# First forward block of a convolution kernel: zeros multiplied while x loads, casts on two engines, two products taken directly in quarters

## The chip, the cores and the metric

The kernel runs on one core of a Trainium2 chip. A core has a matrix engine (TensorE, PE in the profile; its weight loads are PEld), a vector engine (VectorE, DVE), a scalar engine (ScalarE, ACT), a general engine (GpSimd, POOL) and a queue engine that issues DMAs (SyncE, SP). Each works its own list of instructions in order and waits on semaphores for the others. The metric is the device time of one execution in microseconds (us), as the median of the runs.

## The reference

A stride-2 convolution over time, a normalisation over time and a GELU, and the gradients of all of it:

```python
L = (T - K) // 2 + 1                      # x is [2, 16000, 256], w is [31, 256, 256], bf16
h = sum(x[:, i:i + 2 * L:2, :] @ w[i] for i in range(K))
h = (h - mean_over_time(h)) / sqrt(var_over_time(h) + 1e-5)
out = gelu(h * gn_gamma + gn_beta)        # and the gradients of x, w, gamma, beta for grad_out
```

The outputs are `out`, the gradient of x, the gradient of w, and those of gamma and beta. The change touches only the first piece of the forward convolution.

## The kernel before

**The whole.** The program has three parts: the forward convolution (stages F0 to F7: 2 batches, 4 chunks each), the element-wise work and the input gradient (G0 to G7), and the weight gradient (W0 to W8). Each convolution is done with fewer products than its definition has: sums and differences of shifted inputs are multiplied by differences of weights, and the results are added up. A chunk has three branches, called `B_`, `A` and `C_` and worked in this order (`ORDER`); each branch has three products ("leaves") of the same names. A branch's operands are sums of rows of x that DVE makes (`f_sums`, line 468), and its weights are differences of the taps in `w` that DVE makes too (`w_sub`, line 460).

**Two forms of a product.** The direct form is `f_leaf` (line 512): 64 matmuls of 256 columns for a whole leaf (two rows of the output, two halves of the channels, four taps, two parities and two halves of the input channels), and its operand is the sum as it is. The other form has three parts: `f_three_b` (line 524), 16 matmuls with a difference of weights `WD`, after which ACT copies that result negated into the other half of the PSUM tile; and `f_three_ac` (line 540), 32 matmuls onto both halves with one more sum, `third`, as operand. It takes 48 matmuls, one more DVE sum, one more DVE difference of weights, and the ACT copy between its parts.

**The first block** (`f_first`, line 705) is branch `B_` of the first chunk. Nothing is in SBUF when it starts. `x_load` (line 390) loads the odd columns of 272 rows of x as plain rows in three pieces (128, 128 and 16 rows; `rows`), has the 31 taps of `w` loaded by 16 loads (`load_w`, line 439; leaf A's in `load_w(A)`, leaf C's in `load_w(C_)`, each for one half of the input channels, one parity and one of two tap groups), transposes the x rows on PE against an identity matrix (`x_first`, line 412), and loads the even columns with four DMA transposes (`turn`, line 304). In `x_first` PE transposes both pieces of 128 rows into four PSUM tiles, ACT casts each tile to bf16 in one piece of 1024 elements (`put`, line 419), and the 16 rows follow. Then `f_first` makes the weights of branch `B_` (the subtractions `w_sub` in quarters or halves), the sums `la` and `lc` (`second`, line 495), and computes leaf A directly (64 matmuls, in three pieces: a quarter, a quarter and a half) and leaves C and B in the other form (48 each). Three ACT passes (`keep`) and a DVE sum end it. The next branch (`split`, line 653) starts with a sum over all columns of x, the even ones included, and an `f_three_b`.

**What sets the order.** Every operation is recorded in a plan by `add` (line 170): engine, cost, what it reads and writes, and a function that emits it. The plan is emitted in the order of the list `STEPS` (line 39), which holds the differences of successive operation numbers; `order` (line 199) adds them up, and `emit` (line 208) pins the program to that order. So each engine's instructions stand in the order of the list, over the whole program. The planner that wrote the list is not part of the kernel; the costs and slacks handed to `add` are not used at run time. Where several operations are recorded by one helper, the profile shows the helper's line: L509 is every forward matmul, L462 every `w_sub`, L477 every sum in `f_sums`, L422 the casts in `x_first`, L538 the copy in `f_three_b`, L562 the `keep` passes.

Of the kernel before, what the change touches and what calls it, by code (L numbers as in the profile page):

```python
# [13 lines left out]
ALU = mybir.AluOpType  # L14
# [20 lines left out]
def mmt(n):  # L35
    return n / 2400.0 + 0.0025
# [1587 lines left out]
```

## Time and profile before

| | us |
|---|---|
| median of 3 runs | 1102.59 (1102.41 to 1102.68) |
| the profiled execution, its own time | 1101.5 |
| its span from the first instruction to the last | 1099.5 |
| PE busy | 1078.2 (98%) |
| DVE busy | 995.2 (91%) |
| ACT busy | 610.5 (56%) |
| POOL busy | 10.3 (1%) |
| mean granted TensorE clock | 0.999 |

The span is 2.0 us shorter than that execution's time: what lies around the program. In the rows that follow, a timeline row gives the start, the length, the engine, the line, the operation with its tiles and shapes, and how often it stands there in a row; the bracket gives the idle time of the engine before it and what ended it. A row of waits gives the total, the number of times, and the longest. A row of groups gives the count, the busy time, the mean of one in nanoseconds, and the idle time before them. The tile `arena` is all of the kernel's large SBUF storage, and `ps` are the four PSUM tiles (`ring`).

### The profile page before, as it was taken

How to read it: one execution, taken by the hardware profiler on the slowest of the kernel's cores; microseconds unless marked ns; L12 is line 12 of the kernel's file. 1: busy time of each engine (PE TensorE's matmuls, PEld its weight loads, DVE VectorE, ACT ScalarE, POOL GpSimd, SP SyncE). 2: the span in 40 equal slices, each digit the busy share in tenths (PEclk: the TensorE clock that was granted, in tenths of full speed). 3: DMA queues.
4: the chain of work that ended last, by engine and by line, in shares of the span. 5: the costliest groups of instructions: out<-in, count | busy, mean ns of one | idle time of the engine just before them, and what ended most of it. 6: DMA issues, size and time to landing. Idle time of an engine off the chain costs nothing. (4 is left out here: it accounts for less than half of the span.)

```text
span 1099.5 us, 19714 instructions
## 1 busy us (share of the span) xinstructions
PE 1078.2 (98%) x8132; PEld 794.9 (72%) x8132; DVE 995.2 (91%) x1026; ACT 610.5 (56%) x854; POOL 10.3 (1%) x27
## 2 busy tenths in 40 slices
PE   5999999999999999999999999999999999998998
PEld 4888899988888994444444444444478888887887
DVE  5987787899989997999999998989699999999995
ACT  2335444678887649798866676676643323331332
POOL 0000000000001000000000000000000000000000
PEclk9999999999999999999999999999999999999999
DMA  9499989796969698988595999989898565796674
GB/s 233 70 206 271 254 254 259 211 203 164 256 150 195 180 320 284 267 230 280 162 286 165 313 308 345 264 255 314 271 332 208 185 221 168 255 356 224 224 235 135
DMA packets 346892, 261.46 MB, mean 238 GB/s; under 512 B 187702, under 2 KB 315572, under 8 KB 340916
## 3 DMA queue, kind: packets, MB, share of 16 engines
q1 hardware_dynamic: 346612, 260.22, 83.6%
q8 instruction: 63, 1.03, 0.4%
q14 instruction: 25, 0.20, 0.1%
q0 software_dynamic: 192, 0.00, 0.0%
HBM read 120.00 MB, written 94.86 MB: 195 GB/s over the span
## 5 line engine op out<-in xcount | busy, mean ns | idle before, releaser
L509 PE MATMUL ps<-arena 128*128 128x256 bf16 (+3 forms) x3668 | 394.9, 271 | 13.7 <-DVE arena L462 7.1
L1057 PE MATMUL ps<-arena 128*128 128x512 bf16 (+1 forms) x1872 | 400.0, 376 | 0.6 <-ACT ps L1084 0.3
L509 PEld LDWEIGHTS <-arena 128*128 128x128 bf16 x3668 | 358.2, 98 | 50.2 <-DVE arena L462 7.9
L1057 PEld LDWEIGHTS <-arena 128*128 128x128 bf16 x1872 | 183.3, 98 | 216.9 <-issue 1.5
L562 ACT ACTIVATE arena<-ps 128x1024 bf16<-128x1024 f32 x189 | 191.2, 1022 | 243.9 <-PE ps L1348 125.3
L1348 PE MATMUL ps<-arena 128*128 128x256 bf16 x2592 | 283.5, 273 | 2.9 <-DVE arena L1301 2.1
L1348 PEld LDWEIGHTS <-arena 128*128 128x128 bf16 x2592 | 253.4, 98 | 33.1 <-DVE arena L1301 2.5
L477 DVE TENSOR_TENSOR arena<-arena 128x2064 bf16<-128x2064 bf16 (+8 forms) x132 | 164.1, 1266 | 22.2 <-PE ps L509 19.6
L1301 DVE TENSOR_TENSOR arena<-arena 128x4096 bf16<-128x4096 bf16 (+2 forms) x50 | 107.1, 2165 | 0.1
L861 DVE TENSOR_TENSOR arena<-arena 128x2048 bf16<-128x2048 bf16 (+1 forms) x80 | 95.4, 1194 | 4.9 <-ACT arena L853 2.4
L1084 ACT ACTIVATE ps<-ps 128x512 f32<-128x512 f32 x108 | 63.0, 584 | 45.3 <-PE ps L1057 45.0
L1020 DVE TENSOR_TENSOR arena<-arena 128x1032 bf16<-128x1032 bf16 (+7 forms) x111 | 85.0, 795 | 0.5 <-PE ps L1057 0.2
L1099 DVE TENSOR_TENSOR arena<-arena 128x1024 bf16<-128x1024 bf16 (+1 forms) x70 | 63.3, 913 | 16.7 <-ACT arena L562 16.5
L849 ACT ACTIVATE arena<-arena,stats 128x1024 bf16<-128x1024 bf16 (+1 forms) x64 | 74.6, 1208 | 2.5 <-DVE stats L795 2.5
L1311 DVE TENSOR_TENSOR arena<-arena 128x4096 bf16<-128x4096 bf16 x32 | 72.5, 2283 | 1.3 <-PE ps L1348 1.2
L1243 DVE TENSOR_TENSOR arena<-arena 128x1536 bf16<-128x1536 bf16 (+3 forms) x56 | 62.0, 1122 | 7.0 <-DMA arena<-dnd 4.8
L1420 ACT COPY ps<-ps 128x512 f32<-128x512 f32 x54 | 30.5, 570 | 62.4 <-PE ps L1348 62.4
L1407 DVE TENSOR_TENSOR arena<-arena 128x2048 bf16<-128x2048 bf16 x54 | 63.7, 1216 | 0.0
L462 DVE TENSOR_TENSOR arena<-arena 128x2048 bf16<-128x2048 bf16 (+1 forms) x45 | 51.0, 1147 | 13.4 <-DMA arena<-in_w_dram 10.8
L538 ACT ACTIVATE ps<-ps 128x512 f32<-128x512 f32 x59 | 34.3, 582 | 49.7 <-PE ps L509 49.6
L584 ACT ACTIVATE arena<-ps 128x512 bf16<-128x512 f32 (+1 forms) x64 | 36.9, 582 | 38.7 <-PE ps L509 38.6
L1354 DVE TENSOR_TENSOR arena<-arena 128x1024 bf16<-128x1024 bf16 x75 | 49.0, 682 | 8.7 <-ACT arena L562 8.5
(68 smaller groups left out, 462.3 us busy)
## 6 DMA issues: line engine op xcount, KB each, us to landing
arena<-in_x_dram SPq DMA_DIRECT2D x28, 1024.0 KB, 8.4
arena<-d2d SPq DMA_DIRECT2D x16, 1216.0 KB, 8.6
out_dram<-arena SPq DMA_DIRECT2D x35, 512.0 KB, 4.9
d2d<-arena SPq DMA_DIRECT2D x30, 384.0 KB, 7.7
arena<-dnd SPq DMA_DIRECT2D x10, 960.0 KB, 7.2
arena<-vl SPq DMA_DIRECT2D x9, 1024.0 KB, 9.7
arena<-in_x_dram SPq DMA_DIRECT2D x32, 256.0 KB, 4.1
hd<-arena SPq DMA_DIRECT2D x8, 1024.0 KB, 5.5
```

Of the source, the lines that this page charges most:

```text
L477: lambda: nc.vector.tensor_tensor(out=o, in0=a, in1=b, op=ALU.add))
L509: yield nc.tensor.matmul(ps[:, dh, cs], lhsT=wt, rhs=mv, start=s0, stop=False, skip_group_check=True)
L562: lambda: nc.scalar.activation(out=out, in_=ps, func=ACT.Copy, scale=scale))
L849: lambda o=o, func=func, i=h[:, dh], sc=sc, bi=bi: SC.activation(out=o, in_=i, func=func, bias=bi, scale=sc))
L861: add("DVE", dve(8 * wd), [o], [a, b_], lambda: V.tensor_tensor(out=o, in0=a, in1=b_, op=op))
L1020: lambda: nc.vector.tensor_tensor(out=o, in0=a, in1=b, op=ALU.add))
L1057: yield nc.tensor.matmul(ps[:, e, 0:wide], lhsT=lt, rhs=mv, start=s0, stop=False, skip_group_check=True)
L1099: add("DVE", dve(o.free_size(), rate), [o], [a, b], lambda: nc.vector.tensor_tensor(out=o, in0=a, in1=b, op=op))
L1301: add("DVE", dve(o.free_size()), outs, ins, lambda: nc.vector.tensor_tensor(out=o, in0=a, in1=b, op=op), kind=kind + " weight_grad")
L1311: add("DVE", dve(4096), [o], [a, b], lambda: nc.vector.tensor_tensor(out=o, in0=a, in1=b, op=ALU.add))
L1348: yield nc.tensor.matmul(ps[:, s, c0:c1], lhsT=lt, rhs=mv, start=s0, stop=False, skip_group_check=True)
L1407: add("DVE", dve(2048), [d4], [d], lambda: nc.vector.tensor_tensor(out=d4, in0=fan(d[:, o0:o0 + 3 * s + 1:s, :], 1, (o1 - o0) * D), in1=fa ...
```

## The change

In the start-up and in `f_first`:

- The tile of zeros `zt2` is set by DVE as the first operation, no longer by POOL. A new helper `idle` multiplies zeros by zeros: eight matmuls of 512 columns at the start of PE's list, before x is there, and six of 512 columns behind the last transposition of x. Their results are not used.
- The casts of the transposed x go in eight pieces of 512 elements, four behind each piece of 128 rows; of each four, three are on ACT and the last on DVE.
- Leaf C is now computed directly as leaf A is (64 matmuls in place of 48, with no `third` and no `WD` for it at this place), and both leaves go in four quarters, one for each half of the input channels and each parity. The subtraction that a quarter needs is a step of its own. The sums `la`, `lc` and the `third` of leaf B are made in two halves each.
- Leaf B keeps the other form.
- `STEPS` is a new list for the whole program (3178 operations, 3164 before). In it x is loaded first, then the weights of leaf A in the pairs that one subtraction needs, then those of leaf C in the same way; the first steps of PE after leaf C are leaf B's `f_three_b`, its `f_three_ac`, and the next branch's `f_three_b` and `f_three_ac`, with no other PE step between.

```diff
+    add("DVE", 0.3, [zt2[:]], [], lambda: nc.vector.memset(zt2[:], 0.0))
     add("DVE", 0.1, [eps_t[:]], [], lambda: nc.vector.memset(eps_t[:], EPS))
...
-    add("POOL", 0.4, [zt2[:]], [], lambda: nc.gpsimd.memset(zt2[:], 0.0))
...
+        def idle(ps, n, cols, fresh, slow):
+            jobs = [(k,) for k in range(n)]
+
+            def go():
+                for _ in jobs:
+                    yield nc.tensor.matmul(ps[:, 0:cols], lhsT=zt2[:, 0:P], rhs=zt2[:, 0:cols], start=fresh, stop=False, skip_group_check=True)
+            return add("PE", n * mmt(cols) * slow, [ps[:, 0:cols]], [zt2[:, 0:cols]], go)
...
         slots = (2, 3, 0, 1)
+        idle(ring[1][:, 1], 8, 512, True, 2.0)
         for g in range(2):
             for j in range(4):
                 for dh in range(2):
-                    pe_turn(ring[slots[j]], dh, [(256 * (r % 2) + P * g, g, P, j, r) for r in (2 * dh, 2 * dh + 1)], g == 0)
-        for j in range(4):
-            ps = ring[slots[j]]
-            k = 4 * (2 * j + 1)
-            put("ACT", flat[:, k:k + 4, 0:256], ps[:].rearrange("p a (r f) -> p (a r) f", r=2))
+                    pe_turn(ring[slots[j]], dh, [(256 * (r % 2) + P * g, g, P, j, r) for r in (2 * dh, 2 * dh + 1)], g == 0, 2.0 - g)
+            for j in range(4):
+                k = 4 * (2 * j + 1)
+                put("DVE" if j == 3 else "ACT", flat[:, k:k + 4, P * g:P * g + P],
+                    ring[slots[j]][:].rearrange("p a (r f) -> p (a r) f", r=2)[:, :, P * g:P * g + P])
         ps = ring[2]
-        pe_turn(ps, 0, [(16 * (4 * j + r), 2, 16, j, r) for j in range(4) for r in range(4)])
+        last = pe_turn(ps, 0, [(16 * (4 * j + r), 2, 16, j, r) for j in range(4) for r in range(4)])
...
+        plan.ops[idle(ring[3][:, 1], 6, 512, True, 1.0)]["preds"].add(last)
...
     def f_first(xt):
-        for sl in (A, C_):
+        ops, third, second = f_sums(xt, 0, 0, B_, 0)
+        for lf in (A, C_):
             for ch in range(2):
-                for v in ([slice(None)] if ch or sl == C_ else [0, 1]):
-                    w_sub(*(W[br][:, sl, ch, :, v] for br in (B_, C_, A)))
-        ops, third, second = f_sums(xt, 0, 0, B_, 0)
-        second(A)
-        second(C_)
+                for par in range(2):
+                    w_sub(*(W[br][:, lf, ch, :, par] for br in (B_, C_, A)))
+            second(lf)
...
-        third(C_, U[2])
-        third(B_, U[1])
         pa, pc, pb = ring[0], ring[1], ring[3]
-        f_leaf(pa, B_, A, ops[A], 0, HM, HM, True, (0,), (0,), 2.0)
-        f_leaf(pa, B_, A, ops[A], 0, HM, HM, False, (0,), (1,))
-        f_leaf(pa, B_, A, ops[A], 0, HM, HM, False, (1,))
-        for ps, lf, u in ((pc, C_, U[2]), (pb, B_, U[1])):
-            f_three_b(ps, B_, lf, ops[lf], 0, HM)
-            f_three_ac(ps, B_, lf, u, 0, HM, HM)
+        for ps, lf in ((pa, A), (pc, C_)):
+            for ch in range(2):
+                for par in range(2):
+                    f_leaf(ps, B_, lf, ops[lf], 0, HM, HM, ch + par == 0, (ch,), (par,))
+        f_three_b(pb, B_, B_, ops[B_], 0, HM)
+        f_three_ac(pb, B_, B_, U[1], 0, HM, HM)
```

The `third(B_, U[1])` now stands behind the differences of branch `B_`. The helper in `f_sums` makes its sums in two halves where the new flag `halves` is set (the first block alone).

More of the change, by code (lines that the diff above doesn't have):

```diff
@@ L412, in x_first, with pe_turn @@
     def x_first(flat, rows):
-        def pe_turn(ps, dh, parts, fresh=True):
+        def pe_turn(ps, dh, parts, fresh=True, slow=1.0):
             jobs = [(dh, slice(c0, c0 + nm), rows[g][0:nm, j, r * P:(r + 1) * P], ident[0:nm, 0:nm], fresh and i == 0)
                     for i, (c0, g, nm, j, r) in enumerate(parts)]
-            f_mm(ps, jobs, [ps[:, dh]], [ident, *(rows[g] for g in sorted({p[1] for p in parts}))], 2.0)
+            return f_mm(ps, jobs, [ps[:, dh]], [ident, *(rows[g] for g in sorted({p[1] for p in parts}))], slow)
+        def idle(ps, n, cols, fresh, slow):
[4 more added lines that the diff above has]
+            return add("PE", n * mmt(cols) * slow, [ps[:, 0:cols]], [zt2[:, 0:cols]], go)
         def put(eng, o, i):
@@ L468, in f_sums @@
     def f_sums(xt, b, c, br, li):
+        halves = (b, c, br) == (0, 0, B_)
         def tt(n, o, a, b, x=0):
@@ L475, in tt @@
                 b = cross(b, 1)
-            add("DVE", dve(o.free_size()), [o], [a, b],
-                lambda: nc.vector.tensor_tensor(out=o, in0=a, in1=b, op=ALU.add))
+            for e in range(2) if halves else (slice(None),):
+                e = slice(e, e + 1) if halves else e
+                p, q, r = o[:, e], a[:, e], b[:, e]
+                add("DVE", dve(p.free_size()), [p], [q, r],
+                    lambda p=p, q=q, r=r: nc.vector.tensor_tensor(out=p, in0=q, in1=r, op=ALU.add))
         if br == B_:
@@ L495, in second @@
         def second(lf):
-            if lf == A and (b, c, br) == (0, 0, B_):
-                for e in range(2):
-                    tt(260, *(v[:, e:e + 1] for v in (la, E0, E1)))
-            elif lf == A:
+            if lf == A:
                 tt(260, la, E0, E1)
@@ L509, in go @@
                 yield nc.tensor.matmul(ps[:, dh, cs], lhsT=wt, rhs=mv, start=s0, stop=False, skip_group_check=True)
-        add("PE", sum(mmt(j[1].stop - j[1].start) for j in jobs) * slow, outs, ins, go)
+        return add("PE", sum(mmt(j[1].stop - j[1].start) for j in jobs) * slow, outs, ins, go)
     def f_leaf(ps, br, lf, op, co, we, wo, fresh, chs=(0, 1), pars=(0, 1), slow=1.0):
@@ L717, in f_first @@
             w_sub(WD[br, B_], v[:, :, 1:4:2], v[:, :, 0:4:2])
+            if br == B_:
+                third(B_, U[1])
         for br in (A, C_, B_):
```

151 rows, old and new, of the table STEPS are left out of this document.

## The prediction

> **What bounds the kernel now.** I read the page's head first, then who waited for whom on PE, then PE's instructions in order of time, then busy time by stretch.
>
> ```profile
> span 1099.5 us, 19714 instructions
> PE 1078.2 (98%) x8132; PEld 794.9 (72%) x8132; DVE 995.2 (91%) x1026; ACT 610.5 (56%) x854; POOL 10.3 (1%) x27
> ```
> ```profile
> PE ps L509 <- DVE arena L462: 7.1, 3, 5.2
> PE ps L509 <- DMA arena<-in_x_dram: 6.3, 2, 4.5
> PE ps L1348 <- DVE arena L1301: 2.1, 1, 2.1
> PE ps L1348 <- DVE arena L1407: 0.8, 1, 0.8
> PE ps L509 <- DVE arena L477: 0.3, 1, 0.3
> PE ps L1057 <- ACT ps L1084: 0.3, 1, 0.3
> PE ps L1057 <- ACT arena L562: 0.3, 1, 0.3
> ```
> ```profile
> 4.53 1.25 PE L509 MATMUL ps<-arena 128*128 128x128 bf16 x10 [4.53 <-DMA arena<-in_x_dram]
> 7.57 3.05 PE L509 MATMUL ps<-arena 128*128 128x128 bf16 x38 [1.79 <-DMA arena<-in_x_dram]
> 15.86 3.60 PE L509 MATMUL ps<-arena 128*128 128x256 bf16 x16 [5.24 <-DVE arena L462]
> 19.82 1.93 PE L509 MATMUL ps<-arena 128*128 128x256 bf16 x16 [0.36 <-DVE arena L462]
> 23.22 56.96 PE L509 MATMUL ps<-arena 128*128 128x256 bf16 x518 [1.48 <-DVE arena L462]
> ```
> ```profile
> 23.22:60.00 36.78, 36.78 (x336) 32.73 (x337) 36.78 (x34) 10.71 (x19) 0.00 (x0) 1.00 0.58 99
> 930.00:1001.00 71.00, 68.14 (x623) 60.47 (x621) 70.90 (x53) 21.09 (x26) 0.00 (x0) 1.00 0.84 289
> ```
>
> PE is busy for 1078.2 of 1099.5 us. Of its 21.3 idle, 4.53 + 1.79 + 5.24 + 0.36 + 1.48 = 13.4 lie before 23.22. After that 2.1 + 0.8 + 3 x 0.3 = 3.8 are waits, and the rest is the end. So from 23.22 on the time is a count of matmuls, and the question is how far PE has come when it first runs without a break. A matmul of 256 columns then takes 56.96/518 = 0.110. The stretch from 23.22 to 60 (its columns are length, then PE, PEld, DVE, ACT, POOL busy) shows DVE just as full: it can become the next bound.
>
> **The mark.** Before, the first block has 64 + 48 + 48 = 160 products, and 32 of them (two groups of 16) are behind PE at 23.22. The other 128 cost 128 x 0.110 = 14.1: PE has worked them off at 37.3 (a few of the next branch run between them, which moves no sum).
>
> **When the first weight pair is there.**
>
> ```profile
> 11.56 1.23 DVE L462 TENSOR_TENSOR arena<-arena 128x2048 bf16<-128x2048 bf16 x1 [9.97 <-DMA arena<-in_w_dram]
> 12.70 1.30 DVE L477 TENSOR_TENSOR arena<-arena 128x1040 bf16<-128x1040 bf16 x2
> 16.67 10.02 DVE L462 TENSOR_TENSOR arena<-arena 128x2048 bf16<-128x2048 bf16 x9 [0.87 <-DMA arena<-in_w_dram]
> ```
> ```profile
> arena<-in_w_dram SPq DMA_DIRECT2D x14, 256.0 KB, 5.6
> arena<-in_x_dram SPq DMA_DIRECT2D x2, 512.0 KB
> arena<-in_w_dram SPq DMA_DIRECT2D x2, 192.0 KB, 5.3
> arena<-in_x_dram SPq DMA_DIRECT2D x1, 64.0 KB, 6.5
> arena<-in_x_dram SPq DMA_TRANSPOSE x4, 4.2
> ```
>
> In the old list the DVE step at 11.56 waits for x (1088 KB) and four weight loads (960 KB), 2048 KB; the one at 16.67 for ten weight loads, 3520 KB. That is 1472 KB in 5.11, 288 KB per us. The new list loads x, then the weights in the pairs that one subtraction needs, leaf A first. The first pair is complete at 1600 KB: 11.56 - 448/288 = 10.0. The last is complete at 5056 KB: 16.67 + 1536/288 = 22.0; the pairs between come every 1.8 (the last half of them a little faster).
>
> **The start of the products.** Leaf A's first quarter needs its subtraction (1024 elements) and both halves of the sum `la`.
>
> ```profile
> L462 DVE TENSOR_TENSOR arena<-arena 128x1024 bf16<-128x1024 bf16 x2 | 1.4, 688 | 0.0
> L477 DVE TENSOR_TENSOR arena<-arena 128x1040 bf16<-128x1040 bf16 x2 | 1.3, 694 | 0.0
> L1099 DVE TENSOR_TENSOR arena<-ps,arena 128x1024 bf16<-128x1024 f32 x24 | 29.2, 1215 | 0.8 <-ACT arena L849 0.6 <-PE ps L1057 0.2
> ```
> ```profile
> 8.21 4.04 ACT L422 CAST arena<-ps 128x1024 bf16<-128x1024 f32 x5 [6.19 <-PE ps L509]
> 28.78 0.58 ACT L538 ACTIVATE ps<-ps 128x512 f32<-128x512 f32 x1 [0.82 <-PE ps L509]
> ```
>
> Two short DVE steps take 1.30 one after the other, 0.61 from start to start: 10.0 + 0.61 + 0.69 + 0.61 = 11.9, and with the handover PE starts at 12.0 instead of 15.86. The casts lie under this: x's second half is in at 7.57, three ACT casts of 512 elements at 0.58 end by about 9.7, the small one by 10.1, against a need at 10.6. The fourth cast, on DVE, no row shows. Half of the 1.215 of a 1024-element step that reads PSUM is 0.61, an ACT cast 0.58, the whole 1.22; I take 0.68. DVE idles there until 10.0, so it costs nothing below 1.3.
>
> **The clock.** The 16 matmuls at 15.86 took 3.60, the next 16 took 1.93: PE comes slow out of a pause of 5.24 and stays fast over pauses of 0.36 and 1.48. This excess of 1.67 goes if the zeros keep PE running. Eight of 512 columns at the slow pace (3.60/16 per 256) last 3.6, from about 1.1 to 4.7, when x lands anyway (4.53); six at the fast pace last 1.3, behind the transposes, to about 10.5. The pause left before 12.0 is 1.5, like the one of 1.48. On the path the first eight cost at most 0.2, ahead of a wait for x of 1.79, so nothing; the last six wait for the remaining transposes and for one cast, and queued behind them on PE is leaf A's first quarter, which is not ready before 12.0. [...]
>
> **The sum.** The block now has 64 + 64 + 48 = 176 products, 19.4 at 0.110: 12.0 + 19.4 = 31.4. The order list adds two stalls. In the old list the second product's `f_three_b` stands between the first's and its `f_three_ac`, and covers the ACT copy that `f_three_ac` needs. Now one product of this form is left, and nothing on PE stands between; nor does it for the next branch's first product, which the old list covers with leftovers. Each stall is the copy of 0.58 and the handovers. From below 0.6, from above 0.9; I take 0.85, since a matmul's own length exceeds its pace by 0.16.
>
> ```profile
> L509 PE MATMUL ps<-arena 128*128 128x256 bf16 (+3 forms) x3668 | 394.9, 271 | 13.7 <-DVE arena L462 7.1
> ```
>
> So the mark is passed at 31.4 + 0.85 = 32.25, 5.05 earlier, and after the second stall the lead is 4.2.
>
> **Does DVE keep up?** A long step costs (10.02 - 0.69)/8 = 1.17. From 10.0 to 22.0 its list holds 13 short (0.61) and 3 long steps, 11.4: full, but paced by the pairs. The last quarter is ready at 22.7; PE wants it at 12.0 + 7 x 16 x 0.110 = 24.3. Then two long steps and `WD[B,B]`, of which one long step lies before 22.0: 25.0, wanted at 26.1. Three more to 28.5 and the sum for branch A.
>
> ```profile
> L477 DVE TENSOR_TENSOR arena<-arena 128x4192 bf16<-128x4192 bf16 x1 | 2.3, 2331 | 0.0
> 17.30 7.04 SPq L308 DMA_TRANSPOSE arena<-in_x_dram  x4
> ```
>
> That is 30.9, wanted at 32.25. It also needs the four transposes of the even columns: their issue ended at 24.34 and they land some 4.2 after issue; the new list puts one 256 KB load ahead of the last, about 1 more: 28.2 to 29.5, inside the margin. (The new list also moves the small x load and two later `x_pre` loads forward on SP; 64 KB are in the sum above, the two come behind the last weight and wait for nothing.) Nine long steps on, at 33.2 + 10.5 = 43.7, stands the third branch's first weight; PE wants it at 45.4. All margins are 1.1 to 1.7: DVE keeps up, but weights 1 us late move everything by 1.
>
> **The rest of the list** is re-sequenced to its end: of the steps behind this block the diff gives another place in their engine's order to 89 of 867 on PE and 468 of 961 on DVE. Of the 3.8 of later waits the three of 0.3 are single handovers; I take 0.3 off. From below that is 3.8, from above one long DVE step per new wait. Sum: 4.2 + 0.3 = 4.5.
>
> **Against which time.** The profiled execution took 1101.5 and the median of the runs is 1102.59, 1.1 more; I take the difference over: 1102.6 - 4.5 = 1098.1. I call within 0.2% (2.2 us) no change.
>
> **Rivals.**
> - *More is won*: the two stalls are shorter than I put them, the weights land 1 sooner for want of mixing with x, the small waits all go: 4.2 + 1 + 0.9 + 0.5 = 6.6, 1096.0. For it: x's tail mixed with weights in the old order. Against it: DMA was full. 0.17.
> - *The clock closes*: zeros don't count, or the pause of 1.5 is enough. 1.67 come back: 1099.8. [...] 0.10.
> - *One or two late waits*: the new DVE order puts a long step ahead of the one PE waits for, 1.2 to 2.3 each: 1099.3 to 1102.7. 0.12.
> - *Slower*: in the stretch 930 to 1001 DVE is busy 70.90 of 71 and PE already lost 2.9. Nothing absorbs a delay there. Three DVE steps of about 2.3 moved ahead of PE's need cost 6.9, from 1098.1 to 1105.0; it decides from 6.7. 0.06.
>
> ```profile
> 998.58 2.29 DVE arena L1301
> ```
>
> **The numbers.** The forecast has 0.55, with 1096.9 to 1099.4 for its own bounds (stalls 0.5, weights 1). Faster by over 0.2%: 0.55 + 0.17 + 0.10 and a third of the late waits, 0.86; same 0.08; slower 0.06. Range 1095.8 to 1100.8: it leaves out the best of the first rival and the worst of the last two.
>
> **What would show it.** PE's first product at 12.0, at 0.110 at once; no wait of PE over 1 between 12 and 60 except two of about 0.85 that the ACT copy of `f_three_b` ends; the long unbroken PE run ending 4 to 5 earlier; PE's waits behind 60 at 3 to 4 in sum. Wrong would be: a first quarter at the slow pace, a first product after 13, a PE wait on DVE between 24 and 46, or new waits in the last 170 us.

## The result, and the profile after

The changed kernel takes 1097.70 us, the median of 6 runs (1097.23 to 1099.23), against 1102.70 (1102.41 to 1106.40) for the kernel before beside it: a ratio of 0.9949, 95% interval 0.9934 to 0.9963. That is 5.0 faster, 0.45%, beyond the 0.2% that the prediction took as the bound. The profiled execution took 1097.28 with a span of 1095.2, against 1101.5 and 1099.5 before.

First the head of the changed kernel's page, busy time of each engine and its instructions:

```profile
span 1095.2 us, 19717 instructions
PE 1080.6 (99%) x8123; PEld 796.9 (73%) x8162; DVE 996.0 (91%) x1033; ACT 608.9 (56%) x855; POOL 9.8 (1%) x26
```

PE's busy time grew by 2.4 (1078.2 before) while the span fell by 4.3: the gain is idle time of PE. (The 39 matmuls fewer than weight loads are missing records. Some groups below show fewer than were issued, such as 5 of the last 6 zeros.) Next, who waited for whom on PE in the changed kernel: microseconds in all, times, the longest. L425 are the zeros, L521 the forward matmuls, L1068 and L1359 those of the two gradients; L365 sets the zeros, L473 subtracts weights, L492 makes the sums of x, L550 is the ACT copy in `f_three_b`, and L1312 is a DVE step of the weight gradient.

```profile
PE ps L1359 <- DVE arena L1312: 2.9, 2, 2.7
PE ps L521 <- DMA arena<-in_x_dram: 1.7, 1, 1.7
PE ps L425 <- DVE zt L365: 1.2, 1, 1.2
PE ps L521 <- DVE arena L492: 1.0, 1, 1.0
PE ps L521 <- ACT ps L550: 0.7, 1, 0.7
PE ps L521 <- DVE arena L473: 0.7, 1, 0.7
PE ps L1068 <- ACT ps L1095: 0.3, 1, 0.3
```

The 7.1 and 6.3 at the head of the old list are gone. In their place stand 1.2 before the first zeros, 1.7 for the second half of x, 1.0 for the first sum and two waits of 0.7. The longest wait is now the late one, 2.7 where it was 2.1. PE in order of time in the changed kernel: start, duration, what, how many, and in brackets the idle time before.

```profile
1.19 3.60 PE L425 MATMUL ps<-zt 128*128 128x512 bf16 x8 [1.19 <-DVE zt L365]
4.59 1.27 PE L521 MATMUL ps<-arena 128*128 128x128 bf16 x16
7.53 1.61 PE L521 MATMUL ps<-arena 128*128 128x128 bf16 x32 [1.66 <-DMA arena<-in_x_dram]
9.09 1.46 PE L425 MATMUL ps<-zt 128*128 128x512 bf16 x5
11.55 15.95 PE L521 MATMUL ps<-arena 128*128 128x256 bf16 x144 [1.01 <-DVE arena L492]
28.24 5.42 PE L521 MATMUL ps<-arena 128*128 128x256 bf16 x48 [0.73 <-ACT ps L550]
34.33 40.92 PE L521 MATMUL ps<-arena 128*128 128x256 bf16 x372 [0.67 <-DVE arena L473]
```

The first product starts at 11.55 and 144 of them take 15.95, 0.111 each: the fast pace from the first one. Two pauses of 0.73 and 0.67 follow. At 34.33 this kernel has 144 + 48 = 192 products behind it. Of the same work the kernel before had 176 (it needs 16 fewer); 32 were done at 23.22, and the other 144 take 144 x 0.110 = 15.84, to 39.06. The lead out of the first block is 39.06 - 34.33 = 4.73. It is read from one execution of each kernel, and the loads do not land at the same time in each: the first DVE step of the old start-up stands at 11.56 here and at 10.98 and 11.04 in two kernels below with the same loads, so up to half a us of it may be chance.

What became of it? PE in order of time near the end, first of the kernel before, then of the changed one; the last line of each is the final unbroken run of 864 matmuls.

```profile
992.57 6.27 PE L1348 MATMUL ps<-arena 128*128 128x256 bf16 x56 [0.79 <-DVE arena L1407]
1000.91 94.49 PE L1348 MATMUL ps<-arena 128*128 128x256 bf16 x864 [2.07 <-DVE arena L1301]
```
```profile
929.23 63.05 PE L1359 MATMUL ps<-arena 128*128 128x256 bf16 x576 [0.21 <-DVE arena L1312]
995.00 96.09 PE L1359 MATMUL ps<-arena 128*128 128x256 bf16 x864 [2.71 <-DVE arena L1312]
```

The final run starts 5.91 earlier, so 1.18 more was won on the way. The listed waits between explain 0.5 of it (3 x 0.3 + 0.79 + 2.07 = 3.76 before, 0.3 + 0.21 + 2.71 = 3.2 after); the other 0.6 is in no listed wait. By the first weight load of each part the lead is 5.23 at the input gradient (408.42 before, 403.19 after) and 5.92 at the weight gradient (808.81, 802.89), and from there to the final run nothing is added. No run has the new first block with the old order behind it, so what re-sequencing the rest of the list is worth is not separated. But the same 864 matmuls then take 96.09 instead of 94.49: 1.60 is given back, which leaves 4.3, the difference of the spans. Busy time by stretch in the changed kernel shows why. The columns are length, PE, PEld, DVE, ACT, POOL, granted clock, DMA share, GB/s.

```profile
991.50:994.90 3.40, 0.79 (x8) 0.46 (x5) 3.40 (x4) 1.17 (x2) 0.00 (x0) 1.00 0.93 283
994.90:998.30 3.40, 3.30 (x16) 2.37 (x17) 3.40 (x3) 0.00 (x0) 0.00 (x0) 0.50 1.04 311
998.30:1005.00 6.70, 6.70 (x63) 5.98 (x62) 6.70 (x6) 2.28 (x4) 0.00 (x0) 1.00 0.29 101
```

In the late wait PE is busy for only 0.79 of 3.40. Just as it resumes, the granted clock falls to 0.50 for 3.4 us, in which 16 matmuls run where some 31 would. The clock closed behind the longer wait, and that costs about as much as the whole excess of 1.67 that the zeros removed at the front. (At the very start the column of the granted clock does not show the slow pace: in the kernel before it reads 1.00 from 15.8 to 19.5, where 16 matmuls took 3.60. There the pace is the evidence.)

Last, DVE in the changed kernel: the cast's DVE piece, the first subtraction, and steps on which the margins hang.

```profile
8.63 0.69 DVE L433 CAST arena<-ps 128x512 bf16<-128x512 f32 x1 [2.04 <-PE ps L521]
9.59 0.69 DVE L473 TENSOR_TENSOR arena<-arena 128x1024 bf16<-128x1024 bf16 x1 [0.26 <-DMA arena<-in_w_dram]
10.19 1.92 DVE L492 TENSOR_TENSOR arena<-arena 128x1040 bf16<-128x1040 bf16 x3
33.10 1.22 DVE L473 TENSOR_TENSOR arena<-arena 128x2048 bf16<-128x2048 bf16 x1
```
```profile
25.11 2.35 DVE L473 TENSOR_TENSOR arena<-arena 128x2048 bf16<-128x2048 bf16 x2
```

The first weight pair is in at 9.59. The step at 25.11 follows `WD[B,B]` (the difference of weights that leaf B's `f_three_b` needs) without a pause, so `WD[B,B]` ended at about 25.2. PE wanted it at 11.55 + 128 x 0.111 = 25.7. The subtraction at 33.10 ends at 34.32, and PE resumes at 34.33: the second stall ends with this step as much as with the ACT copy, 33.70 to 34.28.

### The profile page after: what moved, and what is told of

Its sections match the earlier page's. It is cut to its first block, busy times and chain, and to the rows that moved or that the text cites. A ratio compares the mean times of both kernels' runs of the same rounds, so it can differ in the third digit from the quotient of the medians.

```text
span 1095.2 us, 19717 instructions
## 1 busy us (share of the span) xinstructions
PE 1080.6 (99%) x8123; PEld 796.9 (73%) x8162; DVE 996.0 (91%) x1033; ACT 608.9 (56%) x855; POOL 9.8 (1%) x26
## 4 chain that ended last, share of the span: by engine, by line
PE 86%; DVE 8%; DMA 2%; ACT 2%; issue 1%; SPq 0%; DVEq 0%; ACTq 0%
PE ps L521 35%; PE ps L1068 34%; PE ps L1359 16%; DVE arena L1322 3%; DVE arena L1312 3%; DVE arena L1365 1%; DVE arena L1418 1%; DMA arena<-d2d 1%; DMA arena<-in_x_dram 1%; DMA arena<-in_w_dram 1%; ACT arena L860 0%; SPq L303 0%; ACT arena L574 0%; DVE arena L492 0%; ACT ps L1095 0%
## 5 line engine op out<-in xcount | busy, mean ns | idle before, releaser
L1068 PE MATMUL ps<-arena 128*128 128x512 bf16 (+1 forms) x1834 | 397.5, 377 | 2.3 <-ACT ps L1095 0.3
L521 PE MATMUL ps<-arena 128*128 128x256 bf16 (+3 forms) x3684 | 393.4, 270 | 4.1 <-DMA arena<-in_x_dram 1.7
L521 PEld LDWEIGHTS <-arena 128*128 128x128 bf16 x3684 | 357.9, 98 | 40.4 <-DMA arena<-in_x_dram 2.5
L1068 PEld LDWEIGHTS <-arena 128*128 128x128 bf16 x1872 | 183.3, 98 | 216.2 <-issue 0.6
L1359 PE MATMUL ps<-arena 128*128 128x256 bf16 x2592 | 285.1, 274 | 2.9 <-DVE arena L1312 2.9
L1359 PEld LDWEIGHTS <-arena 128*128 128x128 bf16 x2592 | 254.1, 98 | 34.0 <-DVE arena L1312 3.5
L492 DVE TENSOR_TENSOR arena<-arena 128x2080 bf16<-128x2080 bf16 (+8 forms) x133 | 163.1, 1252 | 11.9 <-PE ps L521 11.1
L1312 DVE TENSOR_TENSOR arena<-arena 128x4096 bf16<-128x4096 bf16 (+2 forms) x50 | 107.3, 2171 | 0.1
L1031 DVE TENSOR_TENSOR arena<-arena 128x1032 bf16<-128x1032 bf16 (+6 forms) x111 | 85.6, 799 | 5.7 <-PE ps L1068 5.6
L550 ACT ACTIVATE ps<-ps 128x512 f32<-128x512 f32 x58 | 33.8, 583 | 53.8 <-PE ps L521 53.2
L623 DVE TENSOR_TENSOR arena<-arena 128x1024 bf16<-128x1024 bf16 (+3 forms) x52 | 43.4, 843 | 17.8 <-ACT arena L596 9.6
L473 DVE TENSOR_TENSOR arena<-arena 128x2048 bf16<-128x2048 bf16 (+1 forms) x48 | 51.4, 1087 | 7.0 <-DMA arena<-in_w_dram 2.9
```

The lines of the kernel that those rows point to most:

```text
L492: lambda p=p, q=q, r=r: nc.vector.tensor_tensor(out=p, in0=q, in1=r, op=ALU.add))
L521: yield nc.tensor.matmul(ps[:, dh, cs], lhsT=wt, rhs=mv, start=s0, stop=False, skip_group_check=True)
L1031: lambda: nc.vector.tensor_tensor(out=o, in0=a, in1=b, op=ALU.add))
L1068: yield nc.tensor.matmul(ps[:, e, 0:wide], lhsT=lt, rhs=mv, start=s0, stop=False, skip_group_check=True)
L1312: add("DVE", dve(o.free_size()), outs, ins, lambda: nc.vector.tensor_tensor(out=o, in0=a, in1=b, op=op), kind=kind + " weight_grad")
L1359: yield nc.tensor.matmul(ps[:, s, c0:c1], lhsT=lt, rhs=mv, start=s0, stop=False, skip_group_check=True)
```

## The experiments

The theory is that of the prediction: load order and quarters bring the first block forward, the zeros save the slow pace, and each stall is an ACT copy without cover. The rivals were that one part alone does it (the zeros, or the casts on two engines), and that DVE stands right behind each stall, so that removing a stall wins nothing. Then came the question of the clock at the end. A ratio is against the kernel before, run beside it on the same chip.

### Without the zeros

```diff
-            jobs = [(k,) for k in range(n)]
+            jobs = []
```

> The changed kernel with neither group of zeros (14 matmuls that nothing uses are left out). Theory: the zeros keep PE's pace, as the prediction has it. Without them leaf A's first 16 matmuls go at the slow pace (3.6 instead of 1.8 us), the start of leaf A stays at 11.5 and the next branch's first f_three_ac starts 1.7 us later than in the changed kernel, at about 36.0 instead of 34.3; time 1099.4. Rival: the transposes of x alone have PE fast by 11.5 (its pause is shorter than in the kernel before), or DVE is late anyway and hides it: under 0.3 us.

Measured: 1099.73 (1097.82 to 1100.99), ratio 0.9977 (0.9965 to 0.9988). PE, then DVE, in order of time in this kernel:

```profile
7.84 2.41 PE L521 MATMUL ps<-arena 128*128 128x128 bf16 x32 [1.49 <-DMA arena<-in_x_dram]
12.33 17.63 PE L521 MATMUL ps<-arena 128*128 128x256 bf16 x144 [2.08 <-DVE arena L492]
36.78 38.40 PE L521 MATMUL ps<-arena 128*128 128x256 bf16 x349 [0.67 <-DVE arena L473]
```
```profile
9.76 0.69 DVE L433 CAST arena<-ps 128x512 bf16<-128x512 f32 x1 [2.69 <-PE ps L521]
10.37 0.68 DVE L473 TENSOR_TENSOR arena<-arena 128x1024 bf16<-128x1024 bf16 x1
```

The 144 products take 1.68 longer: the slow pace, at the price put on it. They also start 0.78 later. Of this 0.31 is x itself, whose second half came in later in this execution (transposes from 7.84 instead of 7.53). For the rest, transposes at the slow pace (2.41 instead of 1.61) make the casts late, and the DVE piece of the casts now stands right ahead of the first subtraction, at 10.37 instead of 9.59. The run behind the stalls starts 2.45 later. Less the 0.31, the zeros are worth some 2.1 by the profile, and 2.0 by the medians (1099.73 against 1097.70): a little more than the 1.67 of the prediction. That is two fifths of the gain by the medians and about half by the ratios.

### The weights in the old order

```diff
+        old = [24, 26, 25, 23, 27, 29, 15, 14, 28, 30, 16, 17, 18, 19, 21, 20]
+        out = [i for i in out if i not in old]
+        at = out.index(11) + 1
+        return out[:at] + old + out[at:]
```

> The changed kernel with its 16 weight loads in the order of the kernel before (x still ahead of them). Theory: leaf A's early start is owed to the order of the loads. The first pair is then complete at 3072 KB instead of 1600 KB, 5.1 us later: leaf A starts at 16.7, and since DVE has its 12 us of steps still ahead of it the unbroken run of PE starts 5 to 7.5 us later; time 1103 to 1105. Rival: the casts of x or DVE bind at the start and the loads have slack: under 2 us later.

Measured: 1103.49 (1102.44 to 1104.15), ratio 1.0008 (0.9999 to 1.0017). PE in order of time:

```profile
16.61 18.64 PE L524 MATMUL ps<-arena 128*128 128x256 bf16 x144 [6.23 <-DVE arena L495]
42.07 33.14 PE L524 MATMUL ps<-arena 128*128 128x256 bf16 x301 [0.67 <-DVE arena L476]
```

The whole gain is gone, with everything else of the change in place. The first product starts at 16.61 instead of 11.55. Behind the pause of 6.23 the products start at the slow pace: 144 take 18.64 instead of 15.95 (the mean granted clock of this execution is 0.996, of the changed kernel's 0.998). The run behind the stalls starts 7.7 later, 5.1 from the weights and 2.7 from the pace. The order of the loads is the largest part, and with a pause of 6.23 behind them the zeros did not keep the fast pace.

### All casts on ACT

```diff
-                put("DVE" if j == 3 else "ACT", flat[:, k:k + 4, P * g:P * g + P],
+                put("ACT", flat[:, k:k + 4, P * g:P * g + P],
```

> The changed kernel with all eight casts of x on ACT. Theory: the casts lie under the weight loads and two engines for them bring nothing: leaf A starts within 0.2 us of 11.55, time within 0.3 us. Rival: the casts are on the path; ACT then needs one cast of 0.5 us more before the last one, and leaf A starts 0.5 us later.

Measured: 1097.75 (1095.58 to 1097.89, 4 runs), ratio 0.9951 (0.9936 to 0.9966). PE in order of time:

```profile
11.40 15.96 PE L521 MATMUL ps<-arena 128*128 128x256 bf16 x144 [1.15 <-DVE arena L492]
34.18 41.03 PE L521 MATMUL ps<-arena 128*128 128x256 bf16 x373 [0.67 <-ACT ps L550]
```

No different: the products start when the weights let them. The second engine for the casts brings nothing here.

### The second product in its old form

The second leaf goes back to `f_three_b` and `f_three_ac`, with its steps placed where their operands are ready.

```diff
-        for ps, lf in ((pa, A), (pc, C_)):
-            for ch in range(2):
-                for par in range(2):
-                    f_leaf(ps, B_, lf, ops[lf], 0, HM, HM, ch + par == 0, (ch,), (par,))
+        for ch in range(2):
+            for par in range(2):
+                f_leaf(pa, B_, A, ops[A], 0, HM, HM, ch + par == 0, (ch,), (par,))
+        third(C_, U[2])
+        f_three_b(pc, B_, C_, ops[C_], 0, HM)
+        f_three_ac(pc, B_, C_, U[2], 0, HM, HM)
```

> The changed kernel with leaf C in the other form again (48 matmuls instead of 64, one more sum and one difference of weights on DVE ahead of it), its ACT copy covered by the other product. Theory: the direct form wins because it can start on quarters, not because of its count: PE idles about 5 us between leaf A and leaf C, saves 1.75 us of matmuls and one stall of 0.7, and DVE is 2.4 us longer on its way: the unbroken run starts 3 to 6 us later, time 1101 to 1104. Rival: 16 matmuls fewer are worth more than the wait: the time falls by 1 to 2 us.

Measured: 1102.10 (1100.99 to 1104.89), ratio 0.9997 (0.9988 to 1.0006). PE in order of time:

```profile
11.86 7.61 PE L533 MATMUL ps<-arena 128*128 128x256 bf16 x64
25.16 14.69 PE L533 MATMUL ps<-arena 128*128 128x256 bf16 x112 [5.69 <-DVE arena L485]
40.51 34.68 PE L533 MATMUL ps<-arena 128*128 128x256 bf16 x315 [0.67 <-DVE arena L485]
```

The form with 16 products fewer is 6.2 later at the run behind the stalls. It can't start on a quarter, and PE pauses for 5.69. The granted clock is at 0.50 from 9.3 to 12.7, under the last transposes, the zeros and the first products, and behind the pause the pace is slow again: 112 products take 14.69, where 112 x 0.111 is 12.4. Sixteen more matmuls (1.76) buy the quarters, and these fill the time in which the weights land. So load order and quarters are not two gains that add up: in these runs, without either all is lost. The steps of this form were placed by hand in the new list; a list planned for it was not run.

### The stalls filled

Work that is ready is put between `f_three_b` and `f_three_ac`, for this block and for the next branch's first product.

```diff
+        for k, other in ((107, 108), (116, 109), (113, 120), (114, 121)):
+            out.remove(k)
+            out.insert(out.index(other) + 1, k)
...
-                third(B_, U[1])
+                third(B_, U[0])
...
-        f_three_ac(pb, B_, B_, U[1], 0, HM, HM)
+        f_three_ac(pb, B_, B_, U[0], 0, HM, HM)
```

> The changed kernel with the two stalls covered: the last piece of leaf C goes behind leaf B's f_three_b, the last piece of leaf B behind the next branch's f_three_b (the two ACT passes behind the copies, leaf B's third in another buffer so that the next one need not wait for it). No work is added or left out. Theory 1: the stalls of 0.73 and 0.67 are on the path and DVE has the predicted margins of over 1 us: the lead grows by 1.3, time 1096.4. Theory 2: DVE is right behind the stalls, and PE then waits for it instead: under 0.5 us is won.

Measured: 1097.55 (1095.61 to 1098.32), ratio 0.9962 (0.9948 to 0.9976). PE in order of time:

```profile
11.79 13.32 PE L524 MATMUL ps<-arena 128*128 128x256 bf16 x120 [1.02 <-DVE arena L495]
25.89 5.45 PE L524 MATMUL ps<-arena 128*128 128x256 bf16 x48 [0.78 <-DVE arena L476]
31.54 43.68 PE L524 MATMUL ps<-arena 128*128 128x256 bf16 x397 [0.20 <-DVE arena L495]
```

The two waits for ACT (1.40) are gone, and two for DVE stand there, 0.78 for `WD[B,B]` and 0.20 for the next branch's sum. 1.40 - 0.98 is about 0.4, and no gain can be told in the runs. This bears out the rival: DVE is close behind the stalls. How close depends on when the weights land. The kernel further below that has this edit and another was profiled twice, and there PE waited 0.53 for `WD[B,B]` once, and the other time for no more than the list leaves out:

```profile
11.67 18.91 PE L526 MATMUL ps<-arena 128*128 128x256 bf16 x168 [1.01 <-DVE arena L497]
```

With the next wait of 0.20 its long run starts at 30.78, 24 products short of the changed kernel's mark, which it passes at 30.78 + 24 x 0.111 = 33.44. On the same chip the changed kernel reached it at 34.46 from a first product at 11.69. So filling the stalls was worth 0.4 to 1.0 in the profiled executions.

### The clock kept open at the end

Eight matmuls of zeros stand ahead of the late wait, into a bank that the next product overwrites.

```diff
+            for ins in self.zeros() if i == 2970 else ():
+                pin(ins)
...
+    def zeros():
+        for _ in range(8):
+            yield nc.tensor.matmul(ring[2][:, 0], lhsT=zt2[:, 0:P], rhs=zt2[:], start=True, stop=False, skip_group_check=True)
```

> The changed kernel with eight matmuls of zeros (512 columns, into a bank that the next product overwrites) put ahead of the product that waits at 992.3 for 2.7 us near the end of the weight gradient. Theory: PE's clock is closed by that wait (the granted clock is 0.98 in the stretch 930 to 1001, and the 864 matmuls behind it take 96.1 us, against 94.5 in the kernel before), and zeros keep it open: the last run of 864 matmuls is back at 94.5, time 1096.1. Rival: the slower tail has another cause, or the zeros cost what they save: within 0.3 us of 1097.7.

Measured: 1096.43 (1095.70 to 1097.61), ratio 0.9955 (0.9942 to 0.9967). PE near the end:

```profile
993.24 1.67 PE L1603 MATMUL ps<-zt 128*128 128x512 bf16 x7
995.90 94.49 PE L1361 MATMUL ps<-arena 128*128 128x256 bf16 x864 [0.99 <-DVE arena L1314]
```

The pause shrinks to 0.99, and the last 864 matmuls are back at 94.49. The final run starts 0.90 later than in the changed kernel's profile (0.24 of it was there at the run behind the stalls already, on the way a wait of 0.2 is new and another is longer by 0.28, and the rest is the zeros). It still ends 0.7 earlier. The ratio alone can't be told from the changed kernel's, 0.9949 above and 0.9951 below.

### The zeros alone, in the kernel before

Matmuls of zeros ahead of the old kernel's first product: eight, then thirteen in a second kernel.

```diff
+            for ins in self.zeros() if i == 82 else ():
+                pin(ins)
...
+    def zeros():
+        for _ in range(8):
+            yield nc.tensor.matmul(ring[0][:, 0], lhsT=zt2[:, 0:P], rhs=zt2[:], start=True, stop=False, skip_group_check=True)
```

> The kernel before with one part of the change alone: eight matmuls of zeros of 512 columns ahead of leaf A's first quarter, in its pause of 5.24 us. Theory: only the pace of the first 16 products changes, 3.6 us becomes 1.9, but DVE's next quarter was ready only 0.4 us after them and the half after it 1.5 us after the second: the time won turns into waits for DVE, and under 0.3 us is left of 1.7. Rival: the pace itself is on the path: 1.7 us less, 1101.0.

Measured: 1102.33 (1100.50 to 1105.07), ratio 1.0005 (0.9995 to 1.0014). PE in order of time:

```profile
11.16 2.76 PE L1592 MATMUL ps<-zt 128*128 128x512 bf16 x6 [0.22 <-issue]
15.38 3.60 PE L511 MATMUL ps<-arena 128*128 128x256 bf16 x16 [1.45 <-DVE arena L464]
22.74 52.47 PE L511 MATMUL ps<-arena 128*128 128x256 bf16 x477 [1.48 <-DVE arena L464]
```

A miss: behind zeros from 10.36 to 13.92 the first 16 products still took 3.60. This run says nothing on what the fast pace would be worth there. With thirteen in place of eight:

> The kernel before with 13 matmuls of zeros of 512 columns ahead of leaf A's first quarter instead of the 8 that left its pace slow, so that PE has no pause before it. Theory: the first 16 products go at the fast pace (1.9 us) for the most part, and PE then waits for DVE about 2 us instead of 0.36, since the next quarter's subtraction ends where it did: the long run of PE starts within 0.3 us of where it did after DVE's step, time within 0.2% of the kernel before. Rival: 1.7 us less.

Measured: 1102.74 (1100.62 to 1105.91), ratio 1.0006 (0.9994 to 1.0018). PE in order of time:

```profile
11.35 3.45 PE L1592 MATMUL ps<-zt 128*128 128x512 bf16 x11 [0.22 <-issue]
15.32 1.93 PE L511 MATMUL ps<-arena 128*128 128x256 bf16 x16 [0.53 <-DVE arena L464]
19.28 2.95 PE L511 MATMUL ps<-arena 128*128 128x256 bf16 x16 [2.04 <-DVE arena L464]
22.73 52.44 PE L511 MATMUL ps<-arena 128*128 128x256 bf16 x474 [0.50 <-DVE arena L464]
```

Now the first 16 take 1.93, and PE then waits 2.04 for DVE where it waited 0.36. The long run starts at 22.73, as in the kernel with eight at 22.74. (The 2.95 is the clock again: it is at 0.50 from 20.0 to 23.4, behind the wait of 2.04.) In the old order the weights and the DVE steps that wait for them bound PE, and the zeros alone win nothing. The rival that the zeros do it all is out.

### Filled stalls and open clock together

This kernel has both edits, that of the filled stalls and that of the clock kept open. It was measured twice, the second time beside the changed kernel itself.

> Both: the two stalls covered and the zeros ahead of the late wait. Theory 1 with the clock theory: 1.3 + 1.6 less than 1097.7, 1094.8. If DVE is right behind: 1095.7. If neither holds: 1097.5.

> The changed kernel itself, unchanged, on one chip together with the next three, so that they can be set against it: 0.995 of the kernel before. [...]

> The two stalls covered and zeros ahead of the late wait, as in the run before of this name, beside the changed kernel on the same chip. Theory: 0.4 to 0.8 us from the stalls (DVE is close behind) and, against those runs in which the clock closes, 1.6 from the zeros: 0.5 to 2.0 us faster than the changed kernel, with less scatter. Rival: no difference beyond 0.3 us.

Measured: 1096.13 (1095.65 to 1096.33), ratio 0.9951 (0.9938 to 0.9963) the first time. The second time 1095.87 (1095.73 to 1096.38), ratio 0.9942 (0.9928 to 0.9955), beside 1097.34 (1096.01 to 1097.75), ratio 0.9951 (0.9937 to 0.9965), for the changed kernel. PE's final run in the kernel with both edits, then in the changed kernel, both from the second time:

```profile
994.63 94.49 PE L1364 MATMUL ps<-arena 128*128 128x256 bf16 x864 [0.99 <-DVE arena L1317]
```
```profile
995.18 96.16 PE L1359 MATMUL ps<-arena 128*128 128x256 bf16 x864 [2.71 <-DVE arena L1312]
```

On one chip the kernel with both is 1.47 faster than the changed kernel (1095.87 against 1097.34), and its runs lie within 0.7 instead of 1.7. Its final run starts 0.55 earlier and is 1.67 shorter in the profiled executions. It is the fastest version of the study. How much of the 1.47 each edit brings was not separated in one comparison.

### Without the last six zeros

```diff
-        plan.ops[idle(ring[3][:, 1], 6, 512, True, 1.0)]["preds"].add(last)
+        plan.ops[idle(ring[3][:, 1], 0, 512, True, 1.0)]["preds"].add(last)
```

> The changed kernel with the first eight matmuls of zeros only (the six behind the transposes are left out). [...] Rival: a pause of 2.5 closes the clock as the late wait of 2.7 does in some runs: 1.7 us more.

Measured: 1097.99 (1096.90 to 1099.09, 7 runs), ratio 0.9958 (0.9946 to 0.9970). Busy time by stretch in this kernel:

```profile
5.70:9.10 3.40, 2.02 (x40) 1.73 (x37) 1.12 (x2) 2.21 (x6) 0.00 (x0) 1.00 1.08 294
9.10:11.62 2.52, 0.08 (x5) 0.01 (x1) 2.24 (x5) 0.74 (x2) 0.00 (x0) 0.51 1.22 290
11.62:16.00 4.38, 4.38 (x21) 3.15 (x22) 4.38 (x8) 0.00 (x0) 0.00 (x0) 0.50 1.22 290
16.00:20.00 4.00, 4.00 (x39) 3.55 (x38) 3.39 (x4) 0.00 (x0) 0.00 (x0) 1.00 1.17 285
```

The clock closes (0.50) at 9.1, where the pause of 2.44 only begins: PE was busy for 2.02 of the 3.4 us up to then. It stays closed to 16.0, and the run behind the stalls starts at 36.48 instead of 34.33. This is not yet a proof for the six zeros: in the changed kernel they start at 9.09, so up to the fall both kernels give PE the same work. The kernel with the second product in its old form has the six, and its clock closed at 9.3 all the same. There it opened again after 3.4 us and not after 6.9:

```profile
9.32:12.73 3.41, 3.19 (x13) 1.47 (x12) 3.22 (x6) 0.73 (x2) 0.00 (x0) 0.50 1.22 290
```

By the profile the rival's price is about right: 144 products took 18.05 instead of 15.95, 2.1 more where it put 1.7. The granted clocks of the runs speak for the six zeros: without them 4 of 7 runs have 0.995 to 0.997, with them 1 of the 12 runs of the changed kernel (0.995, 1099.23). The median is only 0.65 above the changed kernel's 1097.34. In this kernel's profiled execution the late wait did not close the clock (94.49 for the final run); in how many of its other runs it did is not known.

## Why the prediction was right

The time (1098.1 against 1097.7) and the mechanism held: the first product comes 4.3 earlier because the loads and the quarters let it, at the fast pace, and the lead lasts to the end. That the time agrees to 0.4 is in part luck, since misses cancel. By its own steps:

- **First product at 12.0.** It came at 11.55. The pair was there at 9.59 instead of 10.0, 0.4 earlier than 288 KB per us gave. The step was anchored at 11.56 of one execution, and the same loads brought that step at 10.98 and 11.04 in two others, so 0.4 is within the scatter of the loads. The rest of that step held: from the pair to the product it gave 2.0, and 1.96 was measured.
- **The cast on DVE at 0.68.** It took 0.69 and ended at 9.32, under the wait for the first pair, so it cost nothing. Without the zeros it does stand in the way, at 9.76.
- **The clock, 1.67.** 15.95 for 144 products, and 17.63 without zeros: 1.68. The prediction took the zeros as worth the pace alone; they also save some 0.5 by faster transposes ahead of the casts (0.78 less the 0.31 of a later x).
- **Two stalls of 0.85.** They were 0.73 and 0.67, 0.3 less in sum. Their cause is shown for the first; the second ends with a subtraction and the ACT copy within 0.04 of each other, and the profile puts it down to DVE. By the letter this is one of the prediction's signs of being wrong, a wait of PE on DVE between 24 and 46. It cost nothing beyond the copy.
- **DVE keeps up, with margins of 1.1 to 1.7.** It does, but `WD[B,B]` was ready at 25.2, close to the 25.0 forecast, while PE came for it at 25.7 instead of 26.1: a margin of 0.5. For the second stall there is none. With the stalls filled, PE waits 0.2 for the one in all three profiled executions, and 0.78, 0.53 or too little for the list for the other. The margin was right in its own terms (the stalls included) and of no use to anyone who removes them.
- **Lead out of the block, 4.2.** It was 4.73: the earlier start and the shorter stalls add 0.45 + 0.3, and 0.25 goes because 144 products took 15.95 and 48 took 5.42, not 15.84 and 5.28.
- **Later waits 3.8, then 3.5.** The list gives 3.2, and 0.6 more was won outside of it. But the mix isn't what was forecast: the small waits shrank to 0.5, and the late one grew from 2.07 to 2.71. The step left out that a longer late wait can close the clock, at 1.6 to 1.7. So in the profiled execution misses of 0.5 (the lead) and 0.9 (1.18 on the way instead of 0.3) one way stand against 1.6 the other way: 4.3 where the sum said 4.5. This is the luck.
- **Against which time.** The 1.1 from the profiled execution to the median was carried over as if it were the same for both kernels; for the changed kernel it is 0.4 (1097.28 and 1097.70). The profile before is one of high granted clock (0.999), the profile after is one in which the clock closed late (0.998). Of the 20 runs of the kernel before in the last comparison, ten have 0.999 or 1.000 and a median of 1101.27, and ten have 0.998 or less and 1102.88; the changed kernel beside them has 1096.12 (two runs) and 1097.51 (four). Like against like the gain is 5.2 and 5.4, more than the 4.5 of the sum. Where the kernel before loses its 1.6 no profile of it shows.
- **The rivals.** *The clock closes* was right as a price, and in the profiled execution it came at another place: at 994.9, behind the wait of 2.71, and not at 11. That it can close near 9 two variants show (at 9.1 without the last six zeros, at 9.3 with the old form). *Slower* looked to the right stretch (the longest wait is there), but that wait grew by 0.64 and no more.

That the pieces are a chain and no sum is what the experiments add. By the medians, undoing the load order gives back 5.8, the form of the second product 4.4, the zeros 2.0: together 12.2, more than twice the 5.0 won.

## What to carry to other kernels

When loads bound the first stage, order them by the pairs that one step consumes and split the first products so that each starts on what has landed; a form with fewer matmuls that has to wait for all of it lost more here than its 16 matmuls were worth. Keep PE running with zeros up to the first product, try the same in later waits of 2 us and more (behind waits of 2.04 and 2.71 the granted clock fell to 0.50 here), and look at the granted clock behind each such wait, not only at the wait. Before filling a stall, look at what the next engine would be late by: of 1.4 us of stalls 0.4 to 1.0 was to be had.

## What the runs showed of the clock

The wait of 2.7 ahead of the final run closed the clock in three of eight profiled executions (the changed kernel twice, the kernel with the old form once: 96.09, 96.16, 96.16 for the run) and not in the other five (94.49 or 94.50). With it shortened to 0.99 by zeros it did in none of three (94.49), and the wait of 2.07 that the kernel before and its two variants with zeros have there did in none of three either (94.49 or 94.50). Side by side on one chip, the runs of the changed kernel spread from 1096.01 to 1097.75 and those of the kernel with both edits from 1095.73 to 1096.38, which fits a cost of 1.6 to 1.7 that comes in some runs and not in others. The mean granted clock of each run says the same: 0.999 in the two runs at 1096.01 and 1096.23, 0.998 in the four from 1097.29 on, and 0.999 or 1.000 in all six with both edits.

Stretches with the granted clock at 0.50 lasted 3.4 us in the changed kernel (from 994.9, in its second profile from 996.4), in the kernel with the second product in its old form (from 9.3) and in the one with thirteen zeros (from 20.0), and some 6.9 in the kernel without the last six zeros (9.1 to 16.0). In the 3.4 us ahead of these falls PE was busy for 0.79, 1.22 and 1.36 where it ran products (994.9, 996.4, 20.0), and for 1.90 and 2.02 where it ran transposes (9.3, 9.1). Behind the pauses of 5.69 and 6.23 the pace was slow too: 14.69 for 112 products and 18.64 for 144, where 0.111 each makes 12.4 and 16.0. Zeros can bring the fast pace: behind those from 1.19 on, the 32 transposes at 7.53 took 1.61, against 2.41 without. But behind zeros from 10.36 to 13.92 the 16 products at 15.38 took 3.60, and behind zeros from 10.54 to 14.80 those at 15.32 took 1.93. By what rule the clock closes and opens, these runs do not show.
